# Attention and FFN in one kernel: weights decoded as 32-bit words, 1024 a piece, their ranges checked on a second read

## The chip, the cores and the metric

One Trainium2 chip, one NeuronCore. A core has five engines that run their own instruction streams side by side: PE (TensorE, matrix products), DVE (VectorE), ACT (ScalarE), POOL (GpSimd) and SP (SyncE, which here issues all DMA transfers). The metric is the device time of one execution in microseconds (us); lower is better. The kernel before took 712.14 us in the median of 3 runs (711.98 to 712.77).

## What is computed

The inputs q, k and v have 4 batches of 8 heads, 768 positions and 64 features. Each position attends to at most 96 positions behind it and to the first 8; the result, laid out as 3072 rows of 512, goes through a layer norm and a feed-forward network of width 2048:

```python
scores = q @ k^T / 8 - slope[h] * dist;  masked where not (global or local)
x = softmax(scores) @ v                      # heads side by side: 512 per row
xn = (x - mean) / sqrt(var + 1e-6) * g_ln
out = x + max(xn @ w_ch1, 0) @ w_ch2         # 512x2048 and 2048x512
```

The two weights arrive as 64-bit floats. The engines have no 64-bit arithmetic, so the kernel must turn each 8-byte word into a 32-bit float by bit operations, and it then splits that into two 16-bit floats, a high part and a remainder, so that three 16-bit products replace a 32-bit one.

## The kernel before, in words

*Units of work.* A token tile t (0 to 23) is 128 rows. Two tiles make a chunk c (0 to 11, `CT = 2`). `attention` (L169) does a tile: k and q are split into 16-bit parts and transposed by DMA, then for four pairs of heads PE makes scores `s` (L229), DVE adds the mask and takes the row minimum into `T` (L234), ACT does the exponential (L238), DVE casts to the high part `pn` (L243), POOL subtracts for the low part (L244), SP transposes by DMA (L246), PE multiplies with v into `pv` (L253, L254) and DVE reduces (L256). `norm` (L264) ends a tile: statistics on DVE, a power on POOL (L271), the product `xs` on DVE (L274), its split into `xn` on ACT and DVE (L275, L276), a DMA transpose into `xT`.

*The FFN.* `ffn1(c, f)` (L308) multiplies a chunk with block f of the first weight: 12 matmuls (L314 to L316), ReLU on ACT (L318), remainder `h` on DVE (L319). `ffn2(c, n_)` (L322) does the second weight for one tile: 48 matmuls (L328 to L330), the residual on DVE (L334), the store.

*The weights.* `weight` (L138) takes a piece of 128 rows by 512 columns: 32 pieces, 16 of each weight. SP loads it into `st` (three buffers). ACT takes the absolute value of the upper word, read as a 32-bit float, times 2^-111, and sums it into a column of `big` (L146). DVE shifts 16-bit quarters of the word to get the last three mantissa bits (L147), keeps the sign (L148), and joins both with the ACT result shifted left by 3 (L149) into `u`. ACT copies `u` into the high part (L150), POOL subtracts for the low part (L151). The sums in `big` are compared with a bound at the end (L428): they show whether every weight was in the range for which the decode is exact. A flag made from such checks starts a slow general path (`general`), which doesn't run on these inputs.

*Order.* The code first writes tiles 0 and 1 with the first weight's decode and chunk 0's first matmuls, then tile 2, half of the second weight, tile 3, and `ffn1` of chunk 1 with the other half (L384 to L398). Then `run` (L349) writes the FFN of a chunk with the attention of later tiles between. In chunk 3 `extremes` (L408) reduces the decoded weights to their largest values (L412). What is written is then ordered by a list scheduler: it moves instructions of the same engine past each other where their data allow it. `ORDER` (L52 to L56) adds constraints by name: an instruction may not stand ahead of the one it names. Each engine works off its own row of instructions strictly in that order, and SP's row holds all loads, stores and transposes.

## Time and profile before

| what | value |
| --- | --- |
| median of 3 runs | 712.14 us |
| the profiled execution, its own time | 713.68 us |
| its span (first to last instruction) | 711.9 us |
| busy: PE, DVE, ACT, POOL | 595.0, 511.8, 273.0, 208.3 us |
| granted PE clock, mean | 0.986 |
| read from HBM, written | 35.92 MB, 6.29 MB |

The profile is of one execution. Rows of slices cut the span in 40 equal parts, a digit being the busy share in tenths. A row of groups gives line, engine, operation, tile written and read, shapes and count, then busy time and mean ns of one, then the idle time of the engine just ahead of the group and who ended it. A row of the timeline gives start and duration in us. Idle time of an engine costs nothing unless another waits for what it does. Busy PE is matmul records, whose ends are modelled.

### The profile page before, as it was taken

The numbers are of one execution on the slowest core, as the hardware profiler recorded it, in microseconds if no ns is written. First come the engines' busy times: TensorE is split into PE (matmuls) and PEld (weight loads), VectorE is DVE, ScalarE is ACT, GpSimd is POOL, SyncE is SP. The second block draws the span as 40 slices with busy tenths as digits, with TensorE's granted clock in tenths as the row PEclk, the third lists the DMA queues.
The fourth block names the chain that finished last, engine by engine and source line by source line (L and its number), as shares of the span: only waits on it lengthen the run. The fifth ranks groups of instructions, "written<-read, shape, count | busy, mean of one in ns | idle before, by whom it ended". The sixth has DMA issues, their size and how long they took to land. (4 is left out here: it accounts for less than half of the span.)

```text
span 711.9 us, 12401 instructions
## 1 busy us (share of the span) xinstructions
PE 595.0 (84%) x4546; PEld 408.6 (57%) x4546; DVE 511.8 (72%) x1319; ACT 273.0 (38%) x760; POOL 208.3 (29%) x173
## 2 busy tenths in 40 slices
PE   0322658688999989899999989998999999999994
PEld 0211435456657656567667656666677677676662
DVE  4999999989769999876656676677568668561211
ACT  3655764545323534234323423433234334231110
POOL 0453765634313342312212311322122223020000
PEclk9999999899999999999999999999999999999998
DMA  8597877884847579337416556367264263240101
GB/s 207 137 263 182 186 179 214 210 212 97 186 111 117 99 135 182 78 81 149 119 45 125 96 116 125 75 152 166 61 115 89 61 130 78 57 60 16 30 1 34
DMA packets 216132, 85.04 MB, mean 119 GB/s; under 512 B 171904, under 2 KB 208768, under 8 KB 216064
## 3 DMA queue, kind: packets, MB, share of 16 engines
q1 hardware_dynamic: 216064, 84.18, 54.2%
q8 instruction: 37, 0.61, 0.3%
q14 instruction: 31, 0.25, 0.1%
HBM read 35.92 MB, written 6.29 MB: 59 GB/s over the span
## 5 line engine op out<-in xcount | busy, mean ns | idle before, releaser
L314 PE MATMUL f<-xT,w1h 128*128 128x256 f16 x768 | 211.4, 275 | 33.3 <-DVE h L319 31.7
L316 PE MATMUL f<-xT,w1l 128*128 128x256 f16 x768 | 211.6, 276 | 0.0
L315 PE MATMUL f<-xT,w1h 128*128 128x256 f16 x768 | 211.6, 275 | 0.0
L244 POOL TENSOR_TENSOR pn<-T,pn 128x512 f16<-128x512 f32 (+1 forms) x96 | 113.4, 1182 | 246.2 <-DVE pn L243 124.5
L328 PE MATMUL f<-w2h,h 128*128 128x512 f16 x384 | 143.6, 382 | 5.3 <-ACT h L318 2.7
L329 PE MATMUL f<-w2l,h 128*128 128x512 f16 x384 | 144.6, 382 | 1.4 <-POOL w2l L151 1.4
L238 ACT ACTIVATE T<-T,nm 128x256 f32<-128x256 f32 (+1 forms) x192 | 92.1, 480 | 127.8 <-DVE nm L235 122.3
L330 PE MATMUL f<-w2h,h 128*128 128x512 f16 x384 | 140.6, 381 | 0.0
L318 ACT ACTIVATE h<-f 128x256 f16<-128x256 f32 x192 | 70.8, 374 | 159.8 <-PE f L316 158.5
L319 DVE SCALAR_TENSOR_TENSOR h<-f,h 128x256 f16<-128x256 f32 x192 | 79.5, 417 | 65.8 <-ACT h L318 65.1
L315 PEld LDWEIGHTS <-w1h 128*128 128x128 f16 x768 | 75.7, 99 | 57.6 <-issue 37.5
L229 PE MATMUL s<-kT,qT 128*128 128x256 f16 (+1 forms) x384 | 58.4, 280 | 38.7 <-DMA qT<-qn 22.1
L314 PEld LDWEIGHTS <-w1h 128*128 128x128 f16 x768 | 75.8, 99 | 21.1
L316 PEld LDWEIGHTS <-w1l 128*128 128x128 f16 x768 | 75.9, 99 | 9.6
L243 DVE CAST pn<-T 128x512 f16<-128x512 f32 (+1 forms) x88 | 48.0, 547 | 40.2 <-ACT T L238 39.5
L229 PEld LDWEIGHTS <-qT 128*128 128x128 f16 x384 | 36.9, 103 | 56.2 <-DMA qT<-qn 22.3
L234 DVE CUSTOM_DVE_ANT_1 T<-s,mask 128x256 f32<-128x256 f32 x160 | 60.3, 415 | 3.1 <-PE s L229 2.9
L328 PEld LDWEIGHTS <-h 128*128 128x128 f16 x384 | 37.9, 99 | 38.9 <-ACT h L318 3.6
L329 PEld LDWEIGHTS <-h 128*128 128x128 f16 x384 | 37.8, 99 | 36.9 <-issue 2.5
L271 POOL TENSOR_TENSOR rs<-rs,half 128x1 f32<-128x1 f32 x24 | 22.8, 952 | 120.3 <-DVE rs L270 117.8
L253 PE MATMUL pv<-vn,pT 128*128 128x128 f16 x320 | 39.4, 224 | 19.8 <-DMA pT<-pn 19.6
L330 PEld LDWEIGHTS <-h 128*128 128x128 f16 x384 | 37.8, 99 | 31.5 <-issue 3.0
(98 smaller groups left out, 742.3 us busy)
## 6 DMA issues: line engine op xcount, KB each, us to landing
st<-in_moe_w_ch_dram SPq DMA_DIRECT2D x32, 512.0 KB, 4.1
kf<-in_k_dram SPq DMA_DIRECT2D x12, 512.0 KB, 4.6
qf<-in_q_dram SPq DMA_DIRECT2D x12, 512.0 KB, 4.7
vf<-in_v_dram SPq DMA_DIRECT2D x12, 512.0 KB, 4.8
out_dram<-x SPq DMA_DIRECT2D x48, 128.0 KB, 2.4
pT<-pn SPq DMA_TRANSPOSE x96, 3.3
kT<-kn SPq DMA_TRANSPOSE x24, 3.8
qT<-qn SPq DMA_TRANSPOSE x24, 3.9
```

Of the source, the lines that this page charges most:

```text
L229: last = chain(last, pe.matmul(ps[:, u].rearrange("p (two w) -> p two w", two=2), lhsT=qT[:, a * H + h, :], rhs=kT[:, 2 * h:2 * h + 2, :W ...
L234: vec.tensor_tensor_reduce(out=T[:, u, :].rearrange("p (two w) -> p two w", two=2), in0=ps[:, u].rearrange("p (two w) -> p two w", two=2), ...
L238: mk(f"e{t}_{g}", act.activation(out=T[:, u, :], in_=T[:, u, :], func=AF.Exp, scale=-1.0, bias=nm[:, h:h + 1], accum_out=sm[:, h:h + 1]))
L244: pool.tensor_tensor(out=pn[:, :, 1, :], in0=T, in1=pn[:, :, 0, :], op=ALU.subtract)
L314: pe.matmul(ps, lhsT=w1h[:, kk, fs], rhs=xT[:, kk, :], start=(kk == 0), stop=False)
L315: pe.matmul(ps, lhsT=w1h[:, kk, fs], rhs=xT[:, NK + kk, :], start=False, stop=False)
L316: pe.matmul(ps, lhsT=w1l[:, kk, fs], rhs=xT[:, kk, :], start=False, stop=(kk == NK - 1))
L318: mk(f"h{c}_{f}", act.activation(out=hh[:, 0, :], in_=ps, func=AF.Relu))
L319: mk(f"l{c}_{f}", vec.scalar_tensor_tensor(out=hh[:, 1, :], in0=ps, scalar=0.0, in1=hh[:, 0, :], op0=ALU.max, op1=ALU.subtract))
L328: pe.matmul(ps, lhsT=hh[:, 0, tok], rhs=w2h[:, f, :], start=(f == 0), stop=False)
L329: pe.matmul(ps, lhsT=hh[:, 0, tok], rhs=w2l[:, f, :], start=False, stop=False)
L330: pe.matmul(ps, lhsT=hh[:, 1, tok], rhs=w2h[:, f, :], start=False, stop=(f == NF - 1))
```

## The change

The decode works on whole 32-bit words in place, on pieces of 256 rows by 512 columns: 16 pieces of 1024 elements per partition. ACT makes the three last bits from the lower word (a ReLU with scale 2^-29 and a bias that turns rounding into truncation) and writes them over it. DVE joins them with the upper word shifted left by 3, and then combines that with the sign by and and xor. The bit that the shift pushes into the sign's place is always set for weights in range, so the value comes out negated, and the later passes multiply by -2^-120. ACT copies out the high part and DVE makes the low part by multiply and subtract; POOL has no part in it. `u` and the POOL subtraction are gone, and a piece keeps its `st` buffer to the last pass.

The range check is no longer a by-product: `reach` loads each of the 16 pieces again into an `st` buffer, and DVE reduces the top 16 bits of each word, read as 16-bit floats, to the smallest and the largest absolute value. `reaches` writes them beside chunk 4. The norm's `xs` and `xn` move into the rotating buffers of the score tiles `T` (three) and `pn` (three).

```diff
-        st = p3.tile([P, 512], I64, tag="st", name="st" + name, bufs=3)
+        st = p3.tile([P, 2, 512], I64, tag="st", name="st" + name, bufs=3)
...
-        mk("A" + name, act.activation(out=u, in_=hi.bitcast(F32), func=AF.Abs, scale=2.0 ** -111, accum_out=big[:, n:n + 1]))
-        vec.tensor_scalar(out=parts[:, :, 2], in0=parts[:, :, 1], scalar1=13, scalar2=None, op0=ALU.logical_shift_right)
-        vec.tensor_scalar(out=parts[:, :, 3], in0=parts[:, :, 3], scalar1=0x8000, scalar2=None, op0=ALU.bitwise_and)
-        vec.scalar_tensor_tensor(out=ui, in0=ui, scalar=3, in1=hi, op0=ALU.logical_shift_left, op1=ALU.bitwise_or)
-        act.activation(out=dh, in_=u, func=AF.Copy)
-        pool.tensor_tensor(out=dl, in0=u, in1=dh, op=ALU.subtract)
+        mk("A" + name, act.activation(out=lo, in_=words.bitcast(U32).rearrange("p (n two) -> p n two", two=2)[:, :, 0], func=AF.Relu, scale=2.0 ** -29, bias=less))
+        vec.scalar_tensor_tensor(out=lo, in0=hi, scalar=3, in1=lo, op0=ALU.logical_shift_left, op1=ALU.bitwise_or)
+        vec.scalar_tensor_tensor(out=hi, in0=hi, scalar=SIGN, in1=lo, op0=ALU.bitwise_and, op1=ALU.bitwise_xor)
+        u = st.bitcast(F32).rearrange("p a (n two) -> p a n two", two=2)[:, :, :, 1]
+        act.activation(out=dh, in_=u, func=AF.Copy, scale=-2.0 ** -120)
+        vec.scalar_tensor_tensor(out=dl, in0=u, scalar=-2.0 ** -120, in1=dh, op0=ALU.mult, op1=ALU.subtract)
...
+    def reach(src, n):
+        st = p3.tile([P, 2, 512], I64, tag="st", name=f"sr{n}", bufs=3)
+        load.dma_start(out=st, in_=src)
+        top = st.rearrange("p a n -> p (a n)").bitcast(F16).rearrange("p (n four) -> p n four", four=4)[:, :, 3]
+        vec.tensor_reduce(out=low[:, n:n + 1], in_=top, axis=AX.X, op=ALU.min, apply_absolute_value=True)
+        vec.tensor_reduce(out=high[:, n:n + 1], in_=top, axis=AX.X, op=ALU.max, apply_absolute_value=True)
...
-        xs = p1.tile([P, DM], F32, name="xs")
-        xn = p1.tile([P, 2, DM], F16, name="xn")
+        xs = p2.tile([P, DM], F32, tag="T", name=f"xs{t}", bufs=3)
+        xn = p2.tile([P, 2, DM], F16, tag="pn", name=f"xn{t}", bufs=3)
...
+    def reaches(g):
+        for n_ in range(16):
+            reach(piece1(n_ // 2, n_ % 2) if n_ < 8 else piece2(n_ - 8), n_)
+            yield from itertools.islice(g, 3)
+        yield from g
...
-        run(ffn(c), extremes(g) if c == 3 else g, RATE)
+        run(ffn(c), extremes(g) if c == 3 else reaches(g) if c == 4 else g, RATE)
```

The entries of `ORDER` for pieces follow the new numbers of pieces, and constrain nothing of `reach`.

What this does to the rows of the engines is read from the built programs. In the rows below, the new kernel's lines are its own: L152, L153 and L156 are the three DVE passes of the decode, L176 and L177 the two reductions, L147 and L174 the loads; L253, L254, L262, L275 and L338 are what L234, L235, L243, L256 and L319 were.

First, DVE at the decode of the first weight, while tile 1 is under way; before:

```order
L147 TENSOR_SCALAR st_0_3_430<-st_0_3_430 128x512
L148 TENSOR_SCALAR st_0_3_430<-st_0_3_430 128x512
L234 ISA T_3_363,nm<-s_3_364,mask_104 128x256
L234 ISA nm 128x1
L234 ISA T_3_363,nm<-s_3_364,mask_104 128x256
L234 ISA nm 128x1
L235 TENSOR_SCALAR nm<-nm 128x2
L149 SCALAR_TENSOR_TENSOR u_0_3_432<-u_0_3_432,st_0_3_430 128x512
```

and now:

```order
L152 SCALAR_TENSOR_TENSOR st_1_1_491<-st_1_1_491 128x1024
L275 TENSOR_REDUCE x_204<-pv_0_292 128x256
L254 TENSOR_SCALAR nm<-nm 128x2
L295 SCALAR_TENSOR_TENSOR xn_336<-xs_335,rs,xn_336 128x512
L254 TENSOR_SCALAR nm<-nm 128x2
L153 SCALAR_TENSOR_TENSOR st_1_1_491<-st_1_1_491 128x1024
L152 SCALAR_TENSOR_TENSOR st_2_0_562<-st_2_0_562 128x1024
L262 CAST pn_2_352<-T_2_341 128x2x256
L262 CAST pn_3_377<-T_3_366 128x2x256
L277 TENSOR_SCALAR r<-sm 128x8
L153 SCALAR_TENSOR_TENSOR st_2_0_562<-st_2_0_562 128x1024
L156 SCALAR_TENSOR_TENSOR w1l<-st_1_1_491,w1h 128x2x512
```

Three passes of 512 became three of 1024 on half as many pieces, the last of them the subtraction that POOL did.

Second, DVE where chunk 1's first FFN product ends (the numbered h are its blocks); before:

```order
L319 SCALAR_TENSOR_TENSOR h_12_1387<-f_1_12_1374,h_12_1387 128x256
L256 TENSOR_REDUCE x_1705<-pv_0_1763 128x256
L319 SCALAR_TENSOR_TENSOR h_13_1412<-f_1_13_1399,h_13_1412 128x256
L319 SCALAR_TENSOR_TENSOR h_14_1437<-f_1_14_1424,h_14_1437 128x256
L185 SCALAR_TENSOR_TENSOR qn_2440<-qf_2401,qn_2440 128x16x64
L256 TENSOR_REDUCE x_1705<-pv_2_1825 128x256
L319 SCALAR_TENSOR_TENSOR h_15_1462<-f_1_15_1449,h_15_1462 128x256
L260 TENSOR_TENSOR x_1705<-x_1705,r 128x512
L202 SCALAR_TENSOR_TENSOR vn<-vf_1907,vn 128x16x64
```

and now:

```order
L338 SCALAR_TENSOR_TENSOR h_14_1275<-f_1_14_1262,h_14_1275 128x256
L278 RECIPROCAL r<-r 128x8
L176 TENSOR_REDUCE low<-sr_3790 128x1
L177 TENSOR_REDUCE high<-sr_3790 128x1
L204 SCALAR_TENSOR_TENSOR qn_2267<-qf_2228,qn_2267 128x16x64
L338 SCALAR_TENSOR_TENSOR h_15_1291<-f_1_15_1278,h_15_1291 128x256
L176 TENSOR_REDUCE low<-sr_3794 128x1
L177 TENSOR_REDUCE high<-sr_3794 128x1
L353 SCALAR_TENSOR_TENSOR x_719<-f_2_1553,x_719 128x512
L176 TENSOR_REDUCE low<-sr_3798 128x1
L353 SCALAR_TENSOR_TENSOR x_888<-f_3_1736,x_888 128x512
L177 TENSOR_REDUCE high<-sr_3798 128x1
```

The reductions written beside chunk 4 stand here: the first pair behind chunk 1's fourth h, the last ahead of chunk 2's first.

Third, SP's queue at the same stage, where the last pieces of the second weight were loaded; before:

```order
L141 DMA st_12_1390<-in_moe_w_ch_dram 128x512
L141 DMA st_13_1415<-in_moe_w_ch_dram 128x512
L141 DMA st_14_1440<-in_moe_w_ch_dram 128x512
L109 DMA kf_1903<-in_k_dram 128x8x128
L109 DMA qf_1905<-in_q_dram 128x8x128
L109 DMA vf_1907<-in_v_dram 128x8x128
L246 DMA_TRANSPOSE pT_0_1567<-pn_0_1564 128x8x128
L246 DMA_TRANSPOSE pT_1_1605<-pn_1_1602 128x8x128
```

and now:

```order
L174 DMA sr_3758<-in_moe_w_ch_dram 128x2x512
L357 DMA out_dram<-x_129 64x512 x2
L357 DMA out_dram<-x_204 64x512 x2
L174 DMA sr_3774<-in_moe_w_ch_dram 128x2x512
L174 DMA sr_3778<-in_moe_w_ch_dram 128x2x512
L174 DMA sr_3782<-in_moe_w_ch_dram 128x2x512
L296 DMA_TRANSPOSE xT_1314<-xn_1527 128x8x128
L174 DMA sr_3786<-in_moe_w_ch_dram 128x2x512
```

The second read's loads, 1 MB each, stand in SP's row ahead of transposes of tiles 4 and 5.

More of the change, by code (lines that the diff above doesn't have):

```diff
@@ L14 @@
 I64 = mybir.dt.int64
-U16 = mybir.dt.uint16
+U32 = mybir.dt.uint32
 AF = mybir.ActivationFunctionType
@@ L47 @@
 RATE = 1.6
-ORDER = {f"L{n}{t}": e for n in "kqv" for t, e in ((2, "e1_3"), (4, "D2_8"), (6, "h1_0"))}
-ORDER.update({f"D1_0_{c}": "q1" for c in range(1, NK)})
-ORDER.update({f"A1_0_{c}": "e0_2" for c in range(NK)})
-ORDER.update({"A2_10": "x3", "A2_11": "x3", "A2_12": "h1_0", "A2_13": "h1_0", "A2_14": "h1_4", "A2_15": "h1_4"})
+ORDER = {f"L{n}{t}": e for n in "kqv" for t, e in ((2, "e1_3"), (4, "D2_4"), (6, "h1_0"))}
+ORDER.update({"D1_0_1": "q1", "A1_0_0": "e0_2", "A1_0_1": "e0_2"})
+ORDER.update({"A2_5": "x3", "A2_6": "h1_0", "A2_7": "h1_4"})
 ORDER.update({f"X{n}": f"l{2 + n // 8}_{2 * n % 16}" for n in range(16)})
@@ L134, in banded, with weight @@
     w2l = const.tile([P, NF, DM], F16, name="w2l")
-    big = const.tile([P, 2 * NF], F32, name="big")
+    low = const.tile([P, NF], F32, name="low")
+    high = const.tile([P, NF], F32, name="high")
     wm = const.tile([P, 16], F32, name="wm")
-    def weight(src, dh, dl, name, n):
-        st = p3.tile([P, 512], I64, tag="st", name="st" + name, bufs=3)
+    less = const.tile([P, 1], F32, name="less")
+    pool.memset(less, -0.5001)
+    def weight(src, dh, dl, name):
+        st = p3.tile([P, 2, 512], I64, tag="st", name="st" + name, bufs=3)
@@ L148, in weight @@
-        vec.tensor_scalar(out=parts[:, :, 3], in0=parts[:, :, 3], scalar1=0x8000, scalar2=None, op0=ALU.bitwise_and)
-        vec.scalar_tensor_tensor(out=ui, in0=ui, scalar=3, in1=hi, op0=ALU.logical_shift_left, op1=ALU.bitwise_or)
-        act.activation(out=dh, in_=u, func=AF.Copy)
-        pool.tensor_tensor(out=dl, in0=u, in1=dh, op=ALU.subtract)
+        words = st.rearrange("p a n -> p (a n)")
+        both = words.bitcast(I32).rearrange("p (n two) -> p n two", two=2)
+        lo, hi = both[:, :, 0], both[:, :, 1]
@@ L153, in weights1, with piece1, piece2 @@
+        vec.scalar_tensor_tensor(out=dl, in0=u, scalar=-2.0 ** -120, in1=dh, op0=ALU.mult, op1=ALU.subtract)
+    def piece1(j, c):
+        return w1[2 * c * P:2 * (c + 1) * P, j * 512:(j + 1) * 512].rearrange("(a p) n -> p a n", a=2)
+    def piece2(f):
+        return w2[2 * f * P:2 * (f + 1) * P, :].rearrange("(a p) n -> p a n", a=2)
     def weights1(j, c):
         sl = slice(j * 512, (j + 1) * 512)
-        weight(w1[c * P:(c + 1) * P, sl], w1h[:, c, sl], w1l[:, c, sl], f"1_{j}_{c}", j * NK + c)
+        weight(piece1(j, c), w1h[:, 2 * c:2 * c + 2, sl], w1l[:, 2 * c:2 * c + 2, sl], f"1_{j}_{c}")
@@ L157, in weights2 @@
     def weights2(f):
-        weight(w2[f * P:(f + 1) * P, :], w2h[:, f, :], w2l[:, f, :], f"2_{f}", NF + f)
+        weight(piece2(f), w2h[:, 2 * f:2 * f + 2, :], w2l[:, 2 * f:2 * f + 2, :], f"2_{f}")
+    def reach(src, n):
[4 more added lines that the diff above has]
+        vec.tensor_reduce(out=high[:, n:n + 1], in_=top, axis=AX.X, op=ALU.max, apply_absolute_value=True)
@@ L372, in f1w @@
         for j in js:
-            for kk in range(NK):
+            for kk in range(NK // 2):
                 weights1(j, kk)
@@ L390, in banded @@
     go(tokens(2))
-    for f in range(NF // 2):
+    for f in range(NF // 4):
         weights2(f)
@@ L395, in banded @@
         ffn1(1, f)
-    for f in range(NF // 2, NF):
-        ffn1(1, f)
+    for f in range(NF // 4, NF // 2):
+        ffn1(1, 2 * f)
+        ffn1(1, 2 * f + 1)
         weights2(f)
@@ L426, in banded @@
     vec.tensor_scalar(out=ok[:, 3:4], in0=nl, scalar1=float(NL_MAX), scalar2=None, op0=ALU.is_le)
[L427 to L429 removed]
+    lh = const.tile([P, 2], F32, name="lh")
+    vec.tensor_reduce(out=lh[:, 0:1], in_=low, axis=AX.X, op=ALU.min)
+    vec.tensor_reduce(out=lh[:, 1:2], in_=high, axis=AX.X, op=ALU.max)
+    vec.tensor_scalar(out=ok[:, 4:5], in0=lh[:, 0:1], scalar1=0.5, scalar2=None, op0=ALU.is_ge)
+    vec.tensor_scalar(out=ok[:, 10:11], in0=lh[:, 1:2], scalar1=1.984375, scalar2=None, op0=ALU.is_lt)
     okv = const.tile([P, B * NT], F32, name="okv")
```

9 lines of the change are left out of this document (1 added, 8 removed).

## The prediction

> **What bounds the kernel now.** I read the page first: its 40 slices show two regimes.
>
> ```profile
> span 711.9 us, 12401 instructions
> PE   0322658688999989899999989998999999999994
> DVE  4999999989769999876656676677568668561211
> st<-in_moe_w_ch_dram SPq DMA_DIRECT2D x32, 512.0 KB, 4.1
> ```
>
> DVE is full for the first quarter while PE has gaps; later PE is full. Windows put numbers on that (the busy times stand in the order PE, weight loads, DVE, ACT, POOL; then clock, DMA share, GB/s):
>
> ```profile
> 20.00:150.00 130.00, 68.22 (x470) 44.73 (x469) 126.99 (x252) 75.25 (x197) 71.43 (x52) 0.96 0.78 197
> 150.00:212.00 62.00, 54.77 (x404) 35.88 (x403) 49.16 (x123) 25.01 (x68) 20.00 (x16) 0.97 0.63 139
> 212.00:320.00 108.00, 98.04 (x794) 68.90 (x792) 96.18 (x250) 42.00 (x125) 36.47 (x28) 1.00 0.61 116
> 320.00:660.00 340.00, 329.90 (x2582) 229.74 (x2581) 218.71 (x626) 117.21 (x345) 79.17 (x68) 1.00 0.47 96
> ```
>
> From 20 to 150 us DVE has work for 127.0 of 130 us and PE for 68.2. Behind 320 PE works 329.9 of 340. The border is the start of chunk 2's first FFN matmul, and the waits of PE from 212 to 320 are small:
>
> ```profile
> 209.27 0.27 PE L314 MATMUL f<-xT,w1h 128*128 128x256 f16 x1
> PE f L314 <- DVE h L319: 5.6, 4, 1.8
> PE pv L253 <- DMA pT<-pn: 3.7, 4, 1.4
> ```
>
> So a change to DVE's work ahead of 209.27 moves that matmul, and the end moves with it, less what these 9.3 us of waits give back. The work that the change touches, by form:
>
> ```profile
> L148 DVE TENSOR_SCALAR st<-st 128x512 uint16<-128x512 uint16 x32 | 32.7, 1021 | 0.0
> L147 DVE TENSOR_SCALAR st<-st 128x512 uint16<-128x512 uint16 x32 | 29.3, 915 | 0.4 <-ACT u L146 0.4
> L149 DVE SCALAR_TENSOR_TENSOR u<-u,st 128x512 int32<-128x512 int32 x32 | 26.7, 835 | 0.1
> L151 POOL TENSOR_TENSOR w2l<-u,w2h 128x512 f16<-128x512 f32 x16 | 24.0, 1508 | 22.2 <-ACT w2h L150 22.2
> L151 POOL TENSOR_TENSOR w1l<-u,w1h 128x512 f16<-128x512 f32 x16 | 22.5, 1412 | 19.6 <-ACT w1h L150 19.6
> L412 DVE TENSOR_REDUCE wm<-w1h 128x1 f32<-128x1024 f16 x8 | 9.6, 1196 | 0.0
> L234 DVE CUSTOM_DVE_ANT_1 T<-s,mask 128x256 f32<-128x256 f32 x160 | 60.3, 415 | 3.1 <-PE s L229 2.9
> ```
>
> **Part 1, the decode on DVE: +2 us.** Records of DVE overlap a little, so I cost an instruction by the distance to the next start. The timeline has a piece that ran undisturbed, and a 1024-element instruction with two tensor inputs:
>
> ```profile
> 47.43 0.63 DVE L149 SCALAR_TENSOR_TENSOR u<-u,st 128x512 int32<-128x512 int32 x1
> 47.99 0.73 DVE L147 TENSOR_SCALAR st<-st 128x512 uint16<-128x512 uint16 x1
> 48.51 0.78 DVE L148 TENSOR_SCALAR st<-st 128x512 uint16<-128x512 uint16 x1
> 49.08 0.21 DVE L268 BATCH_NORM_AGGREGATE mv<-st 128x2 f32<-128x6 f32 x1
> 59.43 1.22 DVE L202 SCALAR_TENSOR_TENSOR vn<-vf,vn 64x1024 f16<-64x1024 f32 x1
> 60.57 0.68 DVE L260 TENSOR_TENSOR x<-x,r 128x512 f32<-128x512 f32 x1
> ```
>
> Old: 0.56 + 0.52 + 0.57 = 1.65 us a piece, times 32 = 52.8. New: three passes over 1024 at 1.14, times 16 = 54.7. The word passes are half as many but twice as long, and the subtraction that POOL did is now DVE's third pass. No trace shows an integer pass of 1024 with both inputs and the output strided; undisturbed L149 with one strided input costs the same per element as L202, so 1.14 stands, with +10% (5 us) as upper end.
>
> **Part 2, POOL's 46.5 us go: -24 us.** Beside POOL's work on tiles DVE gets slower:
>
> ```profile
> 41.21 1.63 DVE L260 TENSOR_TENSOR x<-x,r 128x512 f32<-128x512 f32 x1
> 44.28 1.48 POOL L244 TENSOR_TENSOR pn<-T,pn 128x512 f16<-128x512 f32 x1 [0.42 <-POOL w1l L151]
> 44.66 1.70 DVE L148 TENSOR_SCALAR st<-st 128x512 uint16<-128x512 uint16 x1
> 46.16 0.65 DVE L267 BATCH_NORM_STATS2 st<-x 128x6 f32<-128x512 f32 x1
> L147 DVE TENSOR_SCALAR st<-st x32: 698/737/2322, 23.8 to 163.1; 128x512 uint16<-128x512 uint16 x32
> L148 DVE TENSOR_SCALAR st<-st x32: 759/782/2661, 24.3 to 163.7; 128x512 uint16<-128x512 uint16 x32
> L149 DVE SCALAR_TENSOR_TENSOR u<-u,st x32: 632/692/1639, 26.7 to 167.4; 128x512 int32<-128x512 int32 x32
> ```
>
> L148 took 1.50 us to the next start beside a POOL subtraction of 1.48, against 0.57 alone: 0.93 lost, 0.63 per us of POOL. If all 46.5 us of L151 cost that, 29 us come back. Not all of DVE's work is hit: L234, fed from PSUM, keeps its 415 ns. The lower end is the decode's own loss, by the minima (32 x (0.698 + 0.759 + 0.632) = 66.8 against 88.7 recorded): 21.9, of which L151, 46.5 of POOL's 91.4 us from 20 to 212, has half: 11. I take 24, nearer the upper end, since casts and subtractions are stretched too (L260 above: 1.63 against 0.68).
>
> The Trainium skill (GPSIMD Engine Reference, the table with clock and SBUF interfaces) says that POOL contends with DVE instructions that run in a two-port mode or have two SBUF inputs. By that the passes with two inputs that come in are exposed to the POOL work that stays, and the one-input passes that go were not; by that alone the relief would stand at its lower end and the forecast at 736. The trace disagrees as to the passes that go: L147 and L148 are stretched to 2.3 and 2.7 us, more than L149.
>
> **Part 3, the second read: +36 us on DVE, in the wrong place.** 32 reductions over 1024 f16 words are added. Their nearest row is L412, 1196 ns, and to the next start as below (the first row is for part 4: the transposes of probabilities issued from 150 to 212 us):
>
> ```profile
> pT<-pn SPq DMA_TRANSPOSE x9, 3.2
> 212.29 1.21 DVE L412 TENSOR_REDUCE wm<-w1h 128x1 f32<-128x1024 f16 x1
> 213.41 0.28 DVE L234 CUSTOM_DVE_ANT_0 T<-s,mask 128x128 f32<-128x128 f32 x1
> ```
>
> 1.12 times 32 is 35.8 us. The code writes them beside chunk 4, where DVE works 218.7 of 340 us and they would be nearly free. The order shows that they don't stand there: all 32 lie between the rows h of chunk 1 and the first h of chunk 2, ahead of the border, on the engine that sets it. The last three decode pieces stand among them. Each pair waits for its load; behind it on DVE are queued the rows h of chunk 1, the casts and the scores of token 5, and for those wait PE's second FFN matmul of chunk 1 and SP's transposes.
>
> **Part 4, order and waits: +3, and 0.** Scores and casts of the token after next, which stood behind chunk 2's first h, stand ahead of it now: some seven short instructions and two copies, 3 us. DVE waited 3.0 + 12.8 us in the two windows up to 212; with more to do it should wait less for PE, but the loads of 1 MB share three buffers, each held until its third pass or its second reduction is over, and every load of the second read is queued on SP ahead of transposes. I take that as even, 0, with -13 and +16 as ends. The +16: 16 loads are 16.8 MB; windows 20 to 150 moved 197 GB/s at a share of 0.78, so 253 at full share, 66 us. The window from 150 to 212 was busy with other traffic for 0.63 of 62, 39 us, nine pT transposes among it; between the first and the last of the new loads the order has five, and other traffic in proportion, so I take two thirds, 26. Sum 92, in a stretch of some 76 (from about 150, where the rows h of chunk 1 begin, to the border at 226).
>
> By the Trainium skill (DMA: Bandwidth & Descriptors, Bandwidth) a 1 MB load moves 341 GB/s; that would be 49 + 26 = 75 us, no wait, and a sum lower by some 3 us. No run here shows a 1 MB load yet.
>
> **Parts without a price.** ACT's passes are these:
>
> ```profile
> L146 ACT ACTIVATE u<-st 128x512 f32<-128x512 f32 x32 | 21.1, 660 | 10.6 <-DMA st<-in_moe_w_ch_dram 10.4
> L146 ACT ACTIVATION_READ_ACCUMULATOR u<-st 128x1 f32 x32 | 6.1, 189 | 0.0
> L184 ACT ACTIVATE qn<-qf 128x1024 f16<-128x1024 f32 x12 | 12.6, 1049 | 9.1 <-POOL kn L181 8.6 <-DMA qf<-in_q_dram 0.4
> ```
>
> Two passes of 1024 at L184's 1049 ns are 33.6 us in all; the Abs with its accumulator alone took 27.2. With the copies ACT does less than before and works 75 of 130 us there, so DVE hides it, unless a load that comes late holds up the exponentials queued behind its first pass; L146 waited 10.4 us for loads in all, and that stays inside part 4's upper end. The norm's xs and xn take turns with the score tiles; that is a rival below.
>
> **Sum.** Border: +2 - 24 + 36 + 3 + 0 = +17, to 226. PE has 16 more score matmuls behind it (1.5 us), and of the 9.3 us of waits in chunks 2 and 3 I take 5 back, as DVE enters them further ahead. Net +10.5: span 722.4, the profiled execution 713.7 + 10.5 = 724.2, the median 712.14 + 10.5 = 722.6, which I round to 723. (The profiled execution ran 1.5 over the median, 1.8 of it outside the span.)
>
> **Rivals.**
> *The checks fall into DVE's waits.* DVE waited 12.8 us of 150 to 212. If the reductions fill all of that, the border moves +4, the end -2.5: 709.6; with POOL's relief at 29 rather than 24, 704.6. I call it 707. For it: windows with idle DVE exist there. Against: those were waits for PE's results, and the order puts fixed rows behind them. It decides when over 10.5 us of waits vanish. Chance 0.14.
> *DMA becomes the bound of the second read.* +16 as worked out: 738. For it: three buffers, 92 us of traffic in 76. Against: slices of 1.6 us in the window from 150 to 212 ran faster than 253 GB/s, the first at 326:
>
> ```profile
> GB/s 326 98 243 92 265 150 0 85 85 169 0 0 11 0 74 136 297 241 212 266 226 200 163 166 68 168 191 169 259 64 169 167 118 221 123 215 11 0 0 95
> ```
>
> At that rate the loads would be 51 us and just fit. Chance 0.20.
> *The shared score tiles bind.* A token's third score tile must wait until the norm of the token before has let go of xs, by way of POOL and ACT; 1 us for each of 18 later tokens on PE: 741. Against: DVE has a third of its time free there. Chance 0.06.
> *Reliefs and costs cancel* to within 0.2% (1.4 us, about what a measurement of this kernel can tell from no change): 712. Chance 0.07.
> That the reductions run where the code has them, beside chunk 4, and the decode alone is felt (+2 - 24, an end near 700) is excluded by the order.
>
> **Numbers.** The forecast, 716 to 731 by its own bounds, has 0.53. Faster is the first rival, 0.14; same 0.07; slower 0.79. The range 707 to 741 leaves out half of the first rival and half of the shared-tile one.
>
> **What would show it.** Right: 32 reductions near 1.2 us between 140 and 225 us, DVE full there, L314 of chunk 2 first at about 226, PE full behind it; decode passes near 1.2 us; few DVE records beyond twice their minimum ahead of 140. Wrong: DVE idle over 15 us in the second read with loads as releaser (DMA bound), the border ahead of 209, decode passes far from 1.2, or new waits behind 320.

## The result, and the profile after

The changed kernel takes 748.21 us in the median of 4 runs (746.44 to 750.54), the kernel before 712.06 (711.5 to 712.77): a ratio of 1.051, 95% interval 1.048 to 1.054, so 36 us slower where 10.5 were forecast. The sign was right, the size a third of what came, and the time lies beyond the range of 707 to 741. The profiled execution took 750.54, its span 748.8. One of the runs below, e14, has a profile of a slow execution only (837.22 us against its median of 714.64), so no border is read for it.

The page of the kernel after, its slices:

```profile
span 748.8 us, 12280 instructions
PE   0302589578955999999899998997999989999994
DVE  4999995989897788888557764765766567653211
```

PE now has a dip at the twelfth and thirteenth slice, 206 to 243 us, where it was at nine tenths before. The windows of the kernel after (busy PE, weight loads, DVE, ACT, POOL, then clock, DMA share, GB/s):

```profile
20.00:150.00 130.00, 67.86 (x492) 47.26 (x492) 114.43 (x236) 74.67 (x148) 34.29 (x27) 0.95 0.82 205
150.00:212.00 62.00, 50.58 (x313) 30.68 (x312) 53.49 (x88) 17.96 (x38) 11.47 (x8) 0.89 1.02 302
212.00:320.00 108.00, 88.83 (x687) 61.33 (x686) 87.91 (x221) 33.05 (x101) 22.62 (x21) 0.90 0.62 138
320.00:660.00 340.00, 321.57 (x2490) 221.38 (x2488) 226.56 (x662) 122.95 (x359) 83.73 (x73) 0.99 0.55 102
...
204.00:222.00 18.00, 12.42 (x73) 6.35 (x74) 14.47 (x20) 5.07 (x10) 3.28 (x2) 0.81 1.02 325
222.00:243.00 21.00, 9.14 (x53) 6.57 (x53) 15.65 (x48) 4.89 (x19) 3.66 (x5) 0.51 0.57 151
```

DVE's load from 20 to 150 us fell from 127.0 to 114.4, so some of the relief is there. From 150 to 212 the DMA engines are full (share 1.02). From 222 to 243 the granted clock is 0.51: PE waits, and then works at half speed. Two rows of PE's timeline show the wait and the border:

```profile
230.73 1.01 PE L248 MATMUL s<-kT,qT 128*128 128x128 f16 x8 [12.01 <-DVE nm L253]
...
236.90 0.37 PE L333 MATMUL f<-xT,w1h 128*128 128x256 f16 x1 [1.41 <-DMA xT<-xn]
```

In the 12 us of that gap DVE hardly stands still, and five of the second read's reductions, some 5.6 us, lie in them (PE, weight loads, DVE, ACT, POOL, clock, DMA share, GB/s):

```profile
218.70:230.70 12.00, 0.01 (x1) 0.00 (x0) 11.74 (x23) 1.06 (x2) 0.99 (x1) 0.65 0.85 292
```

The Trainium skill (TensorE: Matmul & The Clock Gate, HAM oscillation) warns of idle gaps of PE over some 3.4 us; the trace agrees, with half the clock for 21 us around the gap of 12.01.

The border, the start of chunk 2's first FFN matmul, moved from 209.27 to 236.90, by 27.6 us (forecast 17). From it to the end of the span it was 502.6 us and is 511.9: 9.2 us more, where the forecast had 6.5 less. The two misses, 10.6 and 15.7, make up the difference. Chunk 4's first FFN matmul divides the second one:

```profile
318.27 0.27 PE L314 MATMUL f<-xT,w1h 128*128 128x256 f16 x1
340.65 0.27 PE L333 MATMUL f<-xT,w1h 128*128 128x256 f16 x1
```

The first row is of the kernel before, the second of the kernel after. Chunks 2 and 3 took 109.0 us and take 103.7, so the 5 us that were to come back there did come. From chunk 4 to the end it was 393.6 us and is 408.1, 14.5 more.

The prices of the new operations were close. DVE's groups in the kernel after, by form:

```profile
L153 DVE SCALAR_TENSOR_TENSOR st<-st 128x1024 int32<-128x1024 int32 x16 | 20.7, 1292 | 0.1
L152 DVE SCALAR_TENSOR_TENSOR st<-st 128x1024 int32<-128x1024 int32 x16 | 20.3, 1271 | 0.8 <-ACT st L151 0.8
L176 DVE TENSOR_REDUCE low<-sr 128x1 f32<-128x1024 f16 x16 | 19.4, 1210 | 2.8 <-DMA sr<-in_moe_w_ch_dram 2.8
L177 DVE TENSOR_REDUCE high<-sr 128x1 f32<-128x1024 f16 x16 | 19.3, 1209 | 0.0
L156 DVE SCALAR_TENSOR_TENSOR w2l<-st,w2h 128x1024 f16<-128x1024 f32 x8 | 12.4, 1547 | 1.0 <-ACT w2h L155 1.0
L156 DVE SCALAR_TENSOR_TENSOR w1l<-st,w1h 128x1024 f16<-128x1024 f32 x8 | 11.0, 1374 | 0.2 <-ACT w1h L155 0.2
```

The decode takes 64.4 us of records against 88.7, the reductions 38.7, and DVE waited for the loads of the second read for 2.8 us only. What waited as well were the transposes behind them on SP: with three 1 MB loads issued from 205.02 us on, SP took 9.39 us to issue the next two (SP's rows, kernel after), the first of them 5.90 us, where no transpose took more than 1.90 from 150 to 212 us before:

```profile
205.02 1.64 SPq L174 DMA_DIRECT2D sr<-in_moe_w_ch_dram  x3
206.71 9.39 SPq L265 DMA_TRANSPOSE pT<-pn  x2
```

### The profile page after: what moved, and what is told of

Read it like the earlier page. It is cut to its first block, busy times and chain, and to the rows that moved or that the text cites. A ratio compares the mean times of both kernels' runs of the same rounds, so it can differ in the third digit from the quotient of the medians.

```text
span 748.8 us, 12280 instructions
## 1 busy us (share of the span) xinstructions
PE 609.0 (81%) x4546; PEld 414.4 (55%) x4546; DVE 515.9 (69%) x1305; ACT 269.8 (36%) x696; POOL 158.1 (21%) x142
## 5 line engine op out<-in xcount | busy, mean ns | idle before, releaser
L333 PE MATMUL f<-xT,w1h 128*128 128x256 f16 x768 | 215.9, 281 | 19.2 <-DVE h L338 10.2
L334 PE MATMUL f<-xT,w1h 128*128 128x256 f16 x768 | 216.3, 282 | 0.0
L335 PE MATMUL f<-xT,w1l 128*128 128x256 f16 x768 | 216.1, 281 | 0.0
L263 POOL TENSOR_TENSOR pn<-T,pn 128x512 f16<-128x512 f32 (+1 forms) x96 | 108.5, 1131 | 213.3 <-DVE pn L262 145.2
L338 DVE SCALAR_TENSOR_TENSOR h<-f,h 128x256 f16<-128x256 f32 x192 | 79.4, 416 | 79.0 <-ACT h L337 78.3
L248 PE MATMUL s<-kT,qT 128*128 128x256 f16 (+1 forms) x384 | 60.0, 290 | 64.3 <-DVE nm L253 31.2
L334 PEld LDWEIGHTS <-w1h 128*128 128x128 f16 x768 | 77.3, 101 | 47.3 <-issue 24.6
L333 PEld LDWEIGHTS <-w1h 128*128 128x128 f16 x768 | 77.6, 101 | 23.5 <-issue 0.3
L248 PEld LDWEIGHTS <-qT 128*128 128x128 f16 x384 | 38.6, 106 | 83.2 <-issue 35.7
L335 PEld LDWEIGHTS <-w1l 128*128 128x128 f16 x768 | 77.5, 101 | 11.4
L262 DVE CAST pn<-T 128x512 f16<-128x512 f32 (+1 forms) x88 | 52.0, 592 | 40.7 <-ACT T L257 39.3
L272 PE MATMUL pv<-vn,pT 128*128 128x128 f16 x320 | 38.7, 224 | 33.1 <-DMA pT<-pn 32.9
L253 DVE CUSTOM_DVE_ANT_1 T<-s,mask 128x256 f32<-128x256 f32 x160 | 59.6, 416 | 2.8 <-PE s L248 2.7
L347 PEld LDWEIGHTS <-h 128*128 128x128 f16 x384 | 37.8, 98 | 41.6 <-issue 4.9
L272 PEld LDWEIGHTS <-pT 128*128 128x128 f16 x352 | 32.8, 101 | 49.7 <-DMA pT<-pn 46.8
L348 PEld LDWEIGHTS <-h 128*128 128x128 f16 x384 | 37.7, 98 | 35.6 <-issue 1.3
```

What stands on the lines that cost most here:

```text
L248: last = chain(last, pe.matmul(ps[:, u].rearrange("p (two w) -> p two w", two=2), lhsT=qT[:, a * H + h, :], rhs=kT[:, 2 * h:2 * h + 2, :W ...
L263: pool.tensor_tensor(out=pn[:, :, 1, :], in0=T, in1=pn[:, :, 0, :], op=ALU.subtract)
L272: last = chain(last, pe.matmul(pv[:, j, :], lhsT=pT[:, (u * 2) * nb + n_, :], rhs=vv[:, h, :], start=(n_ == 0), stop=False))
L333: pe.matmul(ps, lhsT=w1h[:, kk, fs], rhs=xT[:, kk, :], start=(kk == 0), stop=False)
L334: pe.matmul(ps, lhsT=w1h[:, kk, fs], rhs=xT[:, NK + kk, :], start=False, stop=False)
L335: pe.matmul(ps, lhsT=w1l[:, kk, fs], rhs=xT[:, kk, :], start=False, stop=(kk == NK - 1))
```

## The experiments

Three theories stood at the start: (A) the second read costs, and the decode by itself is worth what was forecast; (B) the decode's relief did not come; (C) the shared score tiles cost the time behind the border. Each run has its median, the border, and the time from the border to the end of the span. The border is of one profiled execution. The kernel before was run beside each group of runs on the same chip, with medians of 713.6 to 714.2.

| run | what it is | median us | border | border to end |
| --- | --- | --- | --- | --- |
| before | | 712.06 | 209.3 | 502.6 |
| after | | 748.21 | 236.9 | 511.9 |
| e1 | after, no second read | 729.68 | 215.8 | 513.8 |
| e2 | after, second read in chunks 4, 5 | 745.62 | 210.2 | 533.6 |
| e3 | before, shared tiles | 724.04 | 227.1 | 494.3 |
| e4 | after, loads without reductions | 739.91 | 223.5 | 512.9 |
| e5 | before, new decode alone | 735.71 | 211.8 | 523.6 |
| e6 | e5 and a POOL pass | 743.96 | 227.6 | 514.4 |
| e7 | after, second read spread | 753.43 | 212.0 | 539.5 |
| e8 | e5, second read spread | 746.31 | 211.5 | 533.2 |
| e9 | e5, order of before | 721.35 | 204.7 | 514.6 |
| e10 | before, order of e5 | 725.93 | 216.8 | 507.7 |
| e11 | e1, order of e3 | 717.05 | 207.1 | 507.7 |
| e12 | after, order of e3 | 748.42 | 239.7 | 509.1 |
| e13 | before, tiles 32 bytes on | 726.48 | 212.6 | 512.1 |
| e14 | e9, tiles where before has them | 714.64 | | |
| e15 | e12, loads without reductions | 734.01 | 225.1 | 507.2 |
| e16 | e12, second read spread | 743.47 | 206.3 | 534.4 |
| e17 | before, kT and vn 32 bytes on, tiles behind them 64 | 722.62 | 210.4 | 510.6 |
| e18 | e9, all tiles at multiples of 64 | 718.43 | 205.0 | 512.7 |

### The parts one by one, the scheduler free: e1 to e4

e1, without the second read:

```diff
-        run(ffn(c), extremes(g) if c == 3 else reaches(g) if c == 4 else g, RATE)
+        run(ffn(c), extremes(g) if c == 3 else g, RATE)
...
+    pool.memset(low, 1.0)
+    pool.memset(high, 1.0)
```

> Edit: the changed kernel without its second read (no sr loads, no 32 reductions; low and high are set to 1.0 once, so the range check of the raw weights is left out). Theory A (the second read is what costs, as 38.7 us of reductions placed ahead of chunk 2; the decode by itself brings the contention relief of 24 us that was forecast): chunk 2 starts near 190 us (209 + 2 - 24 + 3) and the time is near 695 us (690 to 702), below the kernel before. Theory B (the second read costs, but the relief did not come, and the shared score tiles cost some 15 us behind chunk 4): chunk 2 starts near 205 and the time is 710 to 722. Theory C (the second read falls into time that is free and the loss is the decode and the tiles): 735 us or more.

e2, the second read held late:

```diff
+ORDER.update({f"R{n}": f"l{4 + n // 8}_{2 * n % 16}" for n in range(16)})
...
-        load.dma_start(out=st, in_=src)
+        mk(f"R{n}", load.dma_start(out=st, in_=src))
```

> Edit: the changed kernel with each of the 16 sr loads held in the scheduler's order behind an l step of chunks 4 and 5 (eight each, as the extremes are held in chunks 2 and 3), so the second read lies where PE is the bound. Theory A (the place of the second read is the cost): chunk 2 starts as in the run without the second read; in chunks 4 and 5 DVE has 38.7 us more in some 100 us where it is busy for some 67, so up to 10 us come back there: 698 to 712 us. Theory B (transfers and reductions cost wherever they lie): 735 us or more. Theory C (decode and tiles are the cost): within 5 us of the run without the second read, both above 730.

e3, the shared tiles in the kernel before:

```diff
-        xs = p1.tile([P, DM], F32, name="xs")
-        xn = p1.tile([P, 2, DM], F16, name="xn")
+        xs = p2.tile([P, DM], F32, tag="T", name=f"xs{t}", bufs=3)
+        xn = p2.tile([P, 2, DM], F16, tag="pn", name=f"xn{t}", bufs=3)
```

> Edit: the kernel before, with the one part alone that xs and xn come out of the buffers of the score tiles T and pn (three each) and not out of buffers of their own. Theory A (the shared tiles cost the some 15 us that the changed kernel loses behind chunk 4): 722 to 730 us, with the loss spread over chunks 4 to 11. Theory B (the tiles cost nothing; the steady loss is the order that the scheduler chose or the clock): 711 to 714 us.

e4, the loads without the reductions:

```diff
-        top = st.rearrange("p a n -> p (a n)").bitcast(F16).rearrange("p (n four) -> p n four", four=4)[:, :, 3]
+        top = st.rearrange("p a n -> p (a n)").bitcast(F16).rearrange("p (n four) -> p n four", four=4)[:, :16, 3]
```

> Edit: the changed kernel with all 16 sr loads, but each of the 32 reductions takes 16 columns and not 1024 (it leaves the rest of the range check out), so DVE is relieved of nearly all of the 38.7 us and the 16 MB stay. Theory A (DVE's reductions set the border): chunk 2 starts 30 us or more earlier than in the changed kernel (near 200 to 207) and the time is 705 to 718 us. Theory B (the transfers set it: transposes queued behind 1 MB loads, DMA full from 150 to 212): chunk 2 starts no earlier than 225 and the time is 735 us or more.

None of the theories came through whole. Without its second read the changed kernel is 18.5 us faster, but still slower than before, 1.022 times (1.017 to 1.027). The late read came out by its theory B: its border is before's (210.2), but it loses 31 us behind it, so a late place alone does not save the time. The loads without the reductions, e4, took theory B's time (739.91), with a border 13.4 us ahead of the changed kernel's. The tiles in e3 cost a factor of 1.015 (1.012 to 1.019), but ahead of the border, and the chunks behind it even gave 8 us back, so the loss behind chunk 4 is not theirs; theory C falls. In each of these runs the scheduler had made another order of all later instructions, though, and what an order is worth was unknown.

### The decode by itself: e5 and e6

e5, the new decode in the old pieces and the old buffers' room (where the last dots stand, the passes of the change follow, on 512 elements):

```diff
-        st = p3.tile([P, 512], I64, tag="st", name="st" + name, bufs=3)
+        st = p3.tile([P, 512], I64, tag="st", name="st" + name, bufs=5)
...
+        both = st.bitcast(I32).rearrange("p (n two) -> p n two", two=2)
+        lo, hi = both[:, :, 0], both[:, :, 1]
...
```

> Edit: the kernel before with the new decode alone: in place, on 32-bit words, in the old pieces of 512 (32 of them, five buffers of 4 KB in the room of the three and four before), subtraction on DVE; xs and xn keep their own buffers, and there is no second read (the range check of the raw weights is left out). Theory A (the decode is worth what the prediction's parts 1, 2 and 4 gave it, and the shared tiles took it away): chunk 2 starts near 190 to 195 us, 693 to 702 us in all. Theory B (the relief of DVE is smaller; from the run without the second read, 729.7, only the 10.3 us that the shared tiles cost in the kernel before come off): 716 to 722 us, slower than before. Theory C (nothing either way): 711 to 714 us.

e6, a POOL pass added to it:

```diff
         vec.scalar_tensor_tensor(out=dl, in0=u, scalar=-2.0 ** -120, in1=dh, op0=ALU.mult, op1=ALU.subtract)
+        pool.tensor_tensor(out=lo.bitcast(F32), in0=u, in1=dh, op=ALU.subtract)
```

> Edit: the run with the decode alone, and in it one more pass on POOL for each of the 32 pieces, an f32 subtraction of the size of the old one, whose result (into the low words, which nothing reads again) is not used. Theory A (POOL's passes slow DVE's beside them, as the prediction's 24 us say): 15 to 25 us slower than the decode alone, with chunk 2 starting that much later. Theory B (they hardly do): within 4 us of it. A cost between, 5 to 14 us, would also hold the longer time that a buffer is kept.

The decode alone was 1.031 (1.025 to 1.037), worse than each expectation: its border is 2.5 us behind before's, and 21 us are lost behind it, where no decode is left. The POOL pass moved the border by 15.8 us and the time by 8.3, between its two theories. DVE's work from 20 to 212 us rose with it from 159.5 to 184.8, first e5, then e6:

```profile
20.00:150.00 130.00, 71.43 (x498) 47.41 (x498) 119.37 (x284) 80.10 (x184) 37.74 (x28) 0.96 0.87 208
150.00:212.00 62.00, 53.60 (x369) 34.22 (x369) 40.14 (x89) 20.72 (x47) 11.43 (x9) 0.94 0.58 123
20.00:150.00 130.00, 62.49 (x412) 40.60 (x412) 127.74 (x253) 72.06 (x159) 65.55 (x50) 0.96 0.78 190
150.00:212.00 62.00, 51.94 (x367) 34.70 (x367) 57.06 (x129) 29.72 (x76) 28.23 (x22) 0.86 0.78 160
```

So DVE's work grows beside POOL's. How much of the border and the time is POOL's is not shown: the buffer is held longer, and the scheduler made another order of e6 than of e5.

### The second read spread thin: e7 and e8

e7 puts two pieces into each of chunks 3 to 10, e8 does so in e5 with four pieces of 512:

```diff
+ORDER.update({f"R{n}": f"l{3 + n // 2}_{8 * n % 16}" for n in range(16)})
...
-        run(ffn(c), extremes(g) if c == 3 else reaches(g) if c == 4 else g, RATE)
+        run(ffn(c), reaches(extremes(g) if c == 3 else g, range(2 * c - 6, 2 * c - 4)) if 3 <= c <= 10 else g, RATE)
```

> Edit: the changed kernel with its second read spread thin: two of the 16 pieces in each of chunks 3 to 10, held behind l steps in the scheduler's order, so that DVE has 4.8 us of reductions more in a chunk of some 50 us. Theory A (the cost comes from bunching): chunk 2 starts near 212 as in the run without the second read, and 729 to 735 us. Theory B (a reduction of 1.2 us stands in the way of PE's next tile wherever it lies, as in the run with the read in chunks 4 and 5, 745.6): 741 to 748 us.

> Edit: the decode alone with all checks back: a second read in 32 pieces of 512, four in each of chunks 3 to 10, held behind l steps; everything that the changed kernel computes is there, xs and xn have their own buffers. Theory A (tiles and bunching were the loss): the time of the decode alone plus at most 6 us, near or below the kernel before. Theory B (64 reductions near 0.65 us cost where they lie): the decode alone plus 12 to 20 us.

e7 lost 24 us against e1, more even than theory B had it, and e8 11 against e5, between its two. Bunching alone was not the cost, as far as runs with different orders can tell.

### The order held: e9 to e12

The order of the instructions written from chunk 0's first output step on is taken from another kernel and held by constraints, engine by engine:

```diff
+    for e, order in TURNS.items():
+        for x, y in zip(order, order[1:]):
+            tc.add_manual_dep(turn[e][y], turn[e][x].name, NOSYNC, reason="order given")
```

> Edit: the run with the decode alone (735.7 us), with all instructions that stand behind the first FFN output step of chunk 0 in the code held, engine by engine, in the order that they have in the kernel before (the scheduler had chosen another one: 406 of 838 places differ on DVE, 77 of 218 on SP). Same work, same buffers. Theory A (the decode is about even, and the 22 us were lost by the order that the scheduler made of it from chunk 2 on): chunk 2 starts near 212 and the time is 712 to 719 us. Theory B (something in the decode itself or in where its buffers lie slows the later chunks): 731 to 738 us.

> Edit: the reverse: the kernel before, nothing of its work changed, with the instructions behind the first FFN output step of chunk 0 held in the order that the scheduler gave them in the run with the decode alone. Theory A (the order is the loss): 725 to 736 us, with chunk 2 starting near 210 as before. Theory B (the order is worth nothing): 711 to 715 us.

> Edit: the changed kernel without its second read (729.7 us), held from the first FFN output step on in the order of the kernel before with shared tiles (724.0 us; its chunks 4 to 11 took 382 us, these 397). Theory A (order): 713 to 720 us, with chunks 4 to 11 near 382. Theory B (not the order): 727 to 731 us.

> Edit: the whole changed kernel, second read included, held from the first FFN output step on in the order of the kernel before with shared tiles; the 16 sr loads and 32 reductions are left to the scheduler. Theory A (the some 15 us behind chunk 4 are the order's, those of the second read stay): 729 to 737 us, with chunks 4 to 11 near 382 us and not 398. Theory B (the loss behind chunk 4 hangs on the decode or the tiles): 745 to 751 us.

The order is worth 12 to 14 us by itself: e5 came down from 735.7 to 721.4 with before's order (2 us above theory A's range), and before went up from 713.7 to 725.9 (1.019, 1.016 to 1.023) with e5's, all work the same, although in e10 7.5 of the 12 us fell ahead of the border. e11, the changed kernel without its second read in e3's order, is at 1.004 (1.002 to 1.006), inside theory A's range. e12 differs from it in the second read and in the places of a few instructions written ahead of the held part; it took theory B's 748.4, as in the scheduler's own order. So the second read costs 31.4 us when the order is held (18.5 by e1, where it was not). From chunk 4's first FFN matmul to the end of the span it took 402.4 us in e11 and 404.5 in e12, and not the 392.0 of e3: the order was not all of that loss. (The expectations' 382 and 397 end at PE's last FFN matmul, some 10 us earlier.) e11's rows:

```profile
20.00:150.00 130.00, 70.00 (x499) 48.10 (x499) 116.59 (x236) 75.66 (x150) 36.21 (x28) 0.95 0.83 212
150.00:212.00 62.00, 55.39 (x405) 36.06 (x403) 42.13 (x110) 22.89 (x57) 13.56 (x12) 0.94 0.60 124
```

From 20 to 212 us DVE has work for 158.7 of 192 there, and had 176.2 before: 17 us less work, and the border came forward by 2.1.

### Where tiles start: e13, e14, e17, e18

e5 still had 12 us behind the border that its order did not explain (e9: 514.6 against 502.6). In e9 a transposed k took 4.8 us to land in the median where it took 3.8, and the list of addresses in the built program shows why that could be: the constant `less` had moved every tile behind it by 32 bytes. e13 does this to the kernel before, with the same instructions in the same order:

```diff
-    half = const.tile([P, 1], F32, name="half")
+    half = const.tile([P, 9], F32, name="half")
     pool.memset(half, -0.5)
+    half = half[:, 0:1]
```

> Edit: the kernel before, with one constant of 4 bytes a partition made 36, so that every tile allocated behind it starts 32 bytes further on; instructions, orders and buffers are the same one by one. Theory A (the 32 bytes slow the transposes, which read and write those tiles: kT 4.8 us to landing and not 3.8, and late chunks 8 and 9 lose 3 us each): 717 to 722 us. Theory B (a start in SBUF makes no difference, the slower transposes of the decode runs came from the decode): within 0.3% of 713, 711 to 715 us.

e14 gives e9 a `less` of 64 bytes, so that all tiles lie modulo 64 where before has them (kT and vn at 32, all others that the transposes read or write at 0):

```diff
-    less = const.tile([P, 1], F32, name="less")
+    less = const.tile([P, 16], F32, name="less")
```

> Edit: the run with the decode alone in the old order (721.4 us), with its new constant made 64 bytes, so that all tiles start at the multiples of 64 at which they start in the kernel before. Theory A (the shift cost that run some 6 us, and the decode by itself gains a little): chunk 2 starts near 200 to 205 and the time is 706 to 715 us. Theory B (no effect of the shift): 719 to 723 us. The prediction's own sum (2 of DVE, 24 of relief, 3 of order, 5 given back) would put it near 695 us.

e17 and e18 put kT and vn at 0 too, by 32 bytes ahead of them (e13's edit) and 32 behind (the constant `ones`), in before and in e14. In the changed kernel they lie at 0 as well, by its `less`, and all other tiles that the transposes read or write too, as in e17.

> Edit: the kernel before with 32 bytes put in ahead of kT and vn and 32 more behind them (two constants made longer), so that kT and vn start at a multiple of 64 as in the changed kernel, and all other tiles still do; instructions and orders are the same. Theory A (a start at 32 modulo 64 costs a tile that a transpose writes): kT lands in less than 3.8 us and the time is 705 to 711 us, better than before. Theory B (what counts is the tiles that are read by the transposes, and qT, pT, xT; kT's start is worth nothing): 711 to 715 us.

> Edit: the decode alone in the old order, all tiles at multiples of 64, kT and vn too (the raw weights' range check is left out). Theory A (the decode is even: POOL's passes gone take some 27 us off DVE's steps ahead of chunk 2, and DVE idles for as much more): 710 to 716 us, chunk 2 starts at 203 to 209, and DVE is idle for more than 35 us between 20 and 212 us where it was idle for 16 before. Theory B (the prediction's: relief moves the border one for one): chunk 2 starts near 190 and 695 us.

32 bytes made the kernel before 1.017 times as long (1.014 to 1.019), 726.5 us, more than theory A had; moving kT and vn alone 1.012 (1.010 to 1.014), the opposite of what theory A of e17 said. DMA rows (line and operation, KB, median us from issue to landing), of before:

```profile
kT<-kn SPq DMA_TRANSPOSE x24, 3.8
qT<-qn SPq DMA_TRANSPOSE x24, 3.9
xT<-xn SPq DMA_TRANSPOSE x24, 2.8
```

of e13:

```profile
kT<-kn SPq DMA_TRANSPOSE x24, 4.6
qT<-qn SPq DMA_TRANSPOSE x24, 4.6
xT<-xn SPq DMA_TRANSPOSE x24, 3.3
```

of e17:

```profile
kT<-kn SPq DMA_TRANSPOSE x24, 4.5
qT<-qn SPq DMA_TRANSPOSE x24, 4.4
xT<-xn SPq DMA_TRANSPOSE x24, 3.1
```

and of the changed kernel, where k lands nearly as fast as before although kT starts at 0:

```profile
kT<-kn SPq DMA_TRANSPOSE x24, 3.9
```

With kT and vn at 32 the new decode alone is at 714.64, 1.0005 times before (0.999 to 1.002), the upper end of e14's theory A; at 0 (e18) it is 718.43, above theory A's 710 to 716 but 4.2 us below e17, the kernel before with the same starts. So at equal starts the decode in old pieces and order is worth 0 to 4 us, and the prediction's sum for it, 695, is out. Where its relief went, e18's rows show:

```profile
20.00:150.00 130.00, 69.03 (x489) 46.12 (x489) 119.40 (x278) 80.34 (x181) 35.09 (x26) 0.99 0.89 216
150.00:212.00 62.00, 56.60 (x424) 37.22 (x422) 44.22 (x116) 23.54 (x61) 14.53 (x12) 0.97 0.59 117
```

```profile
204.98 0.27 PE L327 MATMUL f<-xT,w1h 128*128 128x256 f16 x1
```

DVE works 163.6 us of the 192 and idles for 28.4, where it idled for 15.8: of 12.6 us that it got back, the border got 4.3. Of this idle time 6.4 us are waits for transposed q, 5.6 for ACT's exponentials and 3.5 for scores from PE. e9, e11, e16 and e18 have a held order, the new decode and no second read ahead of the border; they differ in tiles, starts and which order is held, and the border stands at 204.7 to 207.1 in all four. With the scheduler's own order (e1, e2, e5, e7, e8) it stands at 210.2 to 215.8. DVE, idle for so long, does not set it alone there.

### The second read in a held order: e15 and e16

e15 is e4's edit, e16 that of e7, both with e12's order:

> Edit: the changed kernel in the held order of e12 (748.4 us), its 32 reductions cut to 16 columns each (the rest of that check is left out); the 16 sr loads stay. Without the second read the same order took 717.1. Theory A (DVE's 38.7 us are the cost, the prediction's part 3): 717 to 724 us. Theory B (the transfers are, transposes wait behind 1 MB loads): 738 to 748 us. Between them each has its share, read as the difference to 717.1 and 748.4.

> Edit: the whole changed kernel with its second read spread, two pieces in each of chunks 3 to 10 held behind l steps, and all other instructions held in the order of e11 and e12. Theory A (the place ahead of chunk 2 is the cost; where PE is the bound most of it hides): chunk 2 starts near 207 and the time is 720 to 730 us. Theory B (it costs as much anywhere): 742 to 752 us.

e15 stands between its theories: the transfers cost 17.0 us (717.05 to 734.01) and the reductions 14.4 more (to 748.42). The reductions without the transfers were not run, so 14.4 is their price on top of the loads. Of e15, a window, PE's longest wait from 150 to 240 us, and the border:

```profile
150.00:212.00 62.00, 43.93 (x319) 27.93 (x317) 33.19 (x94) 15.96 (x38) 9.78 (x7) 0.91 1.08 325
```

```profile
PE pv L284 <- DMA pT<-pn: 13.7, 2, 12.0
```

```profile
225.12 0.37 PE L345 MATMUL f<-xT,w1h 128*128 128x256 f16 x1 [0.62 <-DMA xT<-xn]
```

DVE has work for 33 of 62 us, the DMA engines have no room, and PE once waits 12.0 us for a transposed pair of probabilities; SP took 8.52 us to issue one transpose there, behind three loads of the second read and one of v. e16 took theory B's 743.5: 26 us more than e11, all behind the border, with the order of all other instructions the same. Its waits of PE from 320 to 660 us:

```profile
PE pv L286 <- DMA pT<-pn: 14.5, 19, 1.8
PE f L347 <- DVE h L352: 13.5, 15, 2.5
```

In e11 the same two took 2.8 and 4.1:

```profile
PE f L344 <- DVE h L349: 4.1, 5, 1.6
PE pv L283 <- DMA pT<-pn: 2.8, 4, 0.9
```

PE waits 34 times in that window against 9, and for 28.0 us against 6.9, which is 21 of the 26 us. That a reduction of 1.2 us ahead of a row h or a cast, and a load ahead of a transpose, hold PE up a little each time is the reading that fits. No version that has all checks came below the kernel before.

## Why the prediction was wrong, by its steps

*Part 1, the decode's passes, +2:* right within its bounds. 1.27 and 1.29 us are recorded for the word passes in the mean, near the 1.2 that was to be seen. The third pass has 1.37 and 1.55; against 1.22, the median of the word passes, that is some 4 us more over its 16, an estimate, inside the 5 that were allowed.

*Part 2, -24, and the sentence that a change to DVE's work ahead of 209.27 moves that matmul:* this is the first step that failed, and less by the size of the relief than by what it was taken to move. DVE's work from 20 to 212 fell by 12.6 us (e18, whose passes of 512 take 0.60 us to the next start where nothing disturbs them, 3 x 0.60 x 32 = 58 us, 5 more than the old) and by 17.4 (e11, pieces of 1024, +2): some 18 to 19 of relief, an estimate, between the ends of 11 and 29. The border moved by 2 to 4, where the forecast had 22 for decode and relief together. The reading that fits is that DVE looked full with 127.0 of 130 us because POOL stretched its work over waits that were there all the same; with the stretch gone, DVE waits (28.4 us in e18). What holds the border near 205 then was not found: PE's waits in e11 are spread over scores, transposes and rows h, and the DMA share from 20 to 150 us, which rose from 0.78 to 0.89 in e18, is a rival that no run tested. The prediction read the Trainium skill (GPSIMD Engine Reference, the table with clock and SBUF interfaces) as putting the relief at its lower end; the measured one lies between that end and the 24. The row also names passes in a two-port mode; whether L147 and L148 ran in one, no trace shows, so their stretch does not contradict it.

*Part 3, +36:* the sum was nearly right (32.5 us of border and 31.4 of time, order held), and that was luck, for its make-up was not. It was put down to DVE alone; transfers have 17.0 us of the time and reductions 14.4 (e15). The mechanism that it named for DVE was there too: PE's gap of 12.01 us lies over 11.74 us of DVE's work, with five reductions in it. Wrong was also that the reductions would be nearly free beside chunk 4: spread over chunks 3 to 10 the second read cost 26 us (e16 against e11), in chunks 4 and 5 it cost 16 (e2 against e1, each in the scheduler's own order). That DVE is idle for a third of a window says little when what is idle is the time between two steps for which PE waits.

*Part 4, order +3, waits 0 within -13 and +16:* the upper end was it, for the transfers by themselves (+18.0 of border in e15 against e11). Part 3 had too much for DVE by about as much as part 4 had too little for the transfers. The traffic sum, 92 us in 76, was the better guide than the slices of 326 GB/s: the stretch moved 302. So the rival of the DMA bound had the right place, but not the sign that was to show it: DVE waited 2.8 us for the loads, and the transposes behind them on SP did much of the waiting. By the prediction's estimate from the bandwidth that the Trainium skill gives (DMA: Bandwidth & Descriptors, Bandwidth; its row is for loads that GpSimd issues, here SP does) the loads would fit without a wait; that the sum would then be 3 us lower is worked out nowhere. The measured waits decide, and loads and transposes together filled the share to 1.02.

*Behind the border, -6.5:* the second step that failed, with the larger miss. The 5 us of waits in chunks 2 and 3 did come back; what failed is that nothing was taken to change behind 320 us, for chunks 4 to 11 took 14.5 us more. The prediction's own sign for it, new waits behind 320, is there: PE's waits for the transposed k from 320 to 660 us, before, e17 and after:

```profile
PE s L229 <- DMA kT<-kn: 1.6, 3, 0.6
PE s L230 <- DMA kT<-kn: 3.3, 2, 2.2
PE s L248 <- DMA kT<-kn: 7.0, 6, 2.4
```

In the kernel before, moving kT and vn to where the changed kernel has them costs 7.9 us behind the border (e17, 510.6 against 502.6), and 8.1 in chunks 4 to 11. That the starts do the same in the changed kernel was not tried on it, but the runs divide by them: chunks 4 to 11 took 392.0 to 396.5 us in the three with kT and vn at 32 modulo 64 (before, e3, e10) and 401.7 to 408.8 in all twelve with them at 0 and no second read behind chunk 2's start (after, e1, e4, e5, e6, e9, e11, e12, e13, e15, e17, e18), whatever their decode, tiles and order. How the starts would act is open, since k lands in 3.9 us after. The scheduler's order has a share, too: e12 is 2.7 us shorter behind the border than the changed kernel, and loses as much ahead of it. And the first 6.0 us behind the border ran at half the clock, in the wake of the gap, which costs some 3.0 us, an estimate:

```profile
236.90:242.90 6.00, 6.00 (x36) 4.53 (x36) 2.73 (x7) 1.35 (x6) 1.34 (x2) 0.50 0.22 44
```

*The rivals:* that the checks vanish in DVE's waits (707) is out. So is that reliefs and costs cancel (712). The shared tiles (741) cost nothing like 1 us a token: e3 lost ahead of the border, with PE once waiting 18.4 us for a transposed pair, and e11 has them and is within 0.6% of the kernel before. The sum at the border by held orders is -2.1 for decode and tiles (forecast -22), +32.5 for the second read and -2.8 for the changed kernel's own order (together forecast +39): +27.6. The misses of +19.9 and -9.3 partly hide each other.

## What to carry to other kernels

An engine that is full because a neighbour stretches its work is not shown to be the bound; take the stretch out of its time and ask what would be late next. A part of a change that makes a list scheduler deal all later work anew, or that moves where tiles start, brought up to 14 us of its own here, so parts are compared with the order held and the addresses equal. Spare time on DVE and DMA is not free time: 16 loads and 38.7 us of reductions, spread over eight chunks in which PE is the bound, came back as 26 us (e16).
